# Moving two scale totals in the attention loop, and the load and split of the experts' second weight, in an attention and mixture-of-experts kernel

## The chip, the cores and the metric

The kernel runs on one core of a Trainium2 chip. The metric is device time in microseconds (us), as the median of several runs. The engines named below are TensorE (PE, with its weight loads as PEld), VectorE (DVE), ScalarE (ACT), GpSimd (POOL) and SyncE (SP); SP computes nothing here and issues most of the DMA transfers. Each engine works through its own list of instructions in order.

## The reference, cut to what matters

Eight batches of eight heads, 576 positions of 64 dimensions. Half of the heads see the last 32 positions, the other half see every 32nd position. The attention output, seen as 4608 tokens of 512 values, goes through a layer of eight experts, each of which takes exactly 576 tokens, in order of their gate logits over all experts.

```python
attn = np.exp(scores - max)                  # scores masked, scale 1/sqrt(64)
x = (attn / (attn.sum(-1) + 1e-9)) @ v       # -> [4608, 512]
logits = x @ w_gate                          # [4608, 8]
for idx in np.argsort(-logits.flatten()):    # best (token, expert) pair first
    tok, e = idx // 8, idx % 8
    if assigned[tok] >= 0 or counts[e] >= 576:
        continue
    assigned[tok] = e
    counts[e] += 1
for e in range(8):
    h = np.maximum(x[assigned == e] @ w1[e], 0.0)   # w1: 512 x 1024
    out[assigned == e] = h @ w2[e]                  # w2: 1024 x 512
```

## The kernel before

The kernel has two parts, one behind the other.

**Attention.** There are 16 units of work: for each batch one for the strided heads and one for the local heads, with two pairs of heads each. One loop of 33 steps (`for i in range(-1, 2 * nu)`, line 626) works on three pairs at a time: it closes the scores of pair i + 1, opens those of pair i + 2, and mixes and normalises pair i. Here the order of the instructions on every engine is that of the code (`tc.manual_schedule()`). The values are scaled by a power of two that comes from the sum of their squares: `square_v` squares them on ScalarE (line 292), `total_v` (line 294) adds them over the partitions with one small matmul into a PSUM bank and reduces it on VectorE, and `scale_v` (line 299) makes the power of two from it with six short VectorE operations. `norm` (line 397) multiplies by this scale. At the steps 2 and 4, for the first two batches, `total_v` and `scale_v` stand between `max_t` and the second `mix` of the step (lines 659 to 661).

**Experts.** For each of the eight experts, in an order that the data set (the expert that fills first is first), the kernel does the following:

- `search` or `rest` finds the expert and the bound of its logits, in seven rounds of short steps that go from VectorE to TensorE and back (lines 817 to 859);
- `weights` (line 976) reads the expert's number and loads both weights as four transfers each, issued on SP (line 985), into one buffer per weight (`wp`, `bufs=1`); the next expert's load of a weight waits until the last reader of that buffer is done;
- the weights are split into two halves of 16 bits: four squares on ScalarE (`square`, line 1000), a sum with one matmul and a few VectorE operations (`scale`, lines 1006 to 1009), then eight cuts, each one operation on ScalarE and one on VectorE (`split`, lines 1018 and 1019);
- `fetch` (line 1156) finds the token numbers (`indices`), gathers five tiles of token rows on POOL's queue (`tokens`, line 1078), halves them on ScalarE and VectorE and transposes them by DMA on SP (`halve`, lines 1067 to 1069);
- `ffn` (line 1185) multiplies: a hidden stage, the product with the first weight (`hidden`, line 1175, with the relu at 1182 and 1183), and an output stage, the product with the second weight (line 1223, and 1217 for the last 64 rows), whose result is scaled (line 1233) and scattered on POOL's queue (line 1234).

While expert k multiplies, the searching, loading, splitting and fetching for the experts behind it run beside it. TensorE's order is written out by hand: each matmul in `ffn` yields its planned nanoseconds, which advance `clock`; other work stands in `chains`, generators that yield the planned time to their next step, and the step is taken when the clock reaches it. Where it holds a matmul, that matmul then stands at that place of TensorE's order. The other engines are ordered by a scheduler, with `urgent` work first. A chain for the weights of an expert starts at `weights`: 4 us, the four squares of the first weight and its scale, then its cuts, with the squares of the second weight between the first four cuts, the second scale behind the sixth, and the cuts of the second weight at the end. When the multiplication of that expert begins, whatever is left of the chain is taken at once (`rush`, and `advance` in the loop at line 1271). Expert 0 has a path of its own.

## Time and profile before

| | |
|---|---|
| median of 3 runs | 678.89 us (674.91 to 679.88) |
| the profiled execution | 676.12 us |
| its span, from the first instruction to the last | 674.4 us |
| first matmul of expert 0's hidden stage | at 220.4 us |
| last matmul of expert 7's output stage | at 663.1 us |
| DMA | 102.40 MB, mean 152 GB/s |

Times in profile rows are microseconds from the span's start. A row of the timeline reads: start, length, engine, line, operation, output tile, input tiles, shapes, count; in brackets stands how long the engine was idle ahead of it and what ended the wait. A row of the table of stretches reads: stretch, length, busy time and count for each engine, granted clock of TensorE, mean busy share of the 16 DMA engines, and GB/s. The names of tiles are those of the code: `xt` holds transposed token rows, `xr` gathered rows, `w` a weight as loaded, `w1h`, `w1l`, `w2h`, `w2l` the halves, `r` and `g` belong to the search, `rv` to the token numbers.

### The profile page before, as it was taken

The numbers are of one execution on the slowest core, as the hardware profiler recorded it, in microseconds if no ns is written. First come the engines' busy times: TensorE is split into PE (matmuls) and PEld (weight loads), VectorE is DVE, ScalarE is ACT, GpSimd is POOL, SyncE is SP. The second block draws the span as 40 slices with busy tenths as digits, with TensorE's granted clock in tenths as the row PEclk, the third lists the DMA queues.
The fourth block names the chain that finished last, engine by engine and source line by source line (L and its number), as shares of the span: only waits on it lengthen the run. The fifth ranks groups of instructions, "written<-read, shape, count | busy, mean of one in ns | idle before, by whom it ended". The sixth has DMA issues, their size and how long they took to land.

```text
span 674.4 us, 19427 instructions
## 1 busy us (share of the span) xinstructions
PE 602.9 (89%) x8125; PEld 394.4 (58%) x8128; DVE 456.9 (68%) x1381; ACT 333.0 (49%) x554; POOL 110.8 (16%) x124
## 2 busy tenths in 40 slices
PE   7789899999847788999899989989989997999993
PEld 4567676776633564476467458447646744746741
DVE  4858787788787787777686786777768648570200
ACT  2555554555303464843851871664384279761210
POOL 2101101111102000500420430240042041211011
PEclk9959999999967799999999999989999999899997
DMA  8888798887406406803921860860491197911010
GB/s 240 200 231 222 209 241 239 246 234 215 137 2 216 129 1 236 209 17 131 268 63 35 299 129 1 286 160 17 174 245 44 67 306 228 240 35 48 1 40 32
DMA packets 76363, 102.40 MB, mean 152 GB/s; under 512 B 41292, under 2 KB 49062, under 8 KB 75763
## 3 DMA queue, kind: packets, MB, share of 16 engines
q1 hardware_dynamic: 68195, 79.61, 41.5%
q0 software_dynamic: 7360, 21.15, 10.4%
q8 instruction: 64, 1.05, 0.6%
q10 hardware_dynamic: 720, 0.39, 0.2%
q14 instruction: 24, 0.20, 0.1%
HBM read 73.60 MB, written 18.87 MB: 137 GB/s over the span
## 4 chain that ended last, share of the span: by engine, by line
PE 46%; issue 16%; DVE 15%; DMA 11%; ACT 6%; POOL 3%; SPq 1%; another core or an unknown queue 0%; POOLq 0%; ACTq 0%; DVEq 0%
PE ph L1175 17%; PE ph L1223 7%; PE po L394 4%; PE spa L351 4%; DMA w<-in_w_dram 4%; DMA xr<-x_scr,idx 2%; DVE w2l L1019 2%; DVE w1l L1019 2%; POOL xr L1078 2%; ACT jk L292 2%; DMA v_s<-in_ns_dram 2%; POOL out_dram L1234 1%; PE spb L469 1%; PE spa L374 1%; ACT w1h L1018 1%
## 5 line engine op out<-in xcount | busy, mean ns | idle before, releaser
L1175 PE MATMUL ph<-xt,w1h 128*128 128x288 f16 (+2 forms) x1024 | 177.9, 289 | 7.0 <-DMA xt<-xg 4.5
L1175 PEld LDWEIGHTS <-w1h 128*128 128x128 f16 x1024 | 97.7, 99 | 38.0 <-issue 8.5
L1175 PE MATMUL ph<-xt,w1l 128*128 128x288 f16 (+2 forms) x512 | 111.8, 289 | 0.0
L1234 POOL DMA_INDIRECT out_dram<-y,idx x40 | 47.8, 1195 | 337.2 <-ACT y L1233 314.6
L1223 PE MATMUL ph<-w2h,hh 128*128 128x512 f16 x256 | 97.8, 382 | 0.0
L1223 PE MATMUL ph<-w2h,hl 128*128 128x512 f16 x256 | 97.7, 382 | 0.0
L1223 PE MATMUL ph<-w2l,hh 128*128 128x512 f16 x256 | 97.5, 381 | 0.0
L1182 ACT ACTIVATE hh<-ph 128x576 f16<-128x576 f32 (+2 forms) x72 | 42.8, 595 | 108.6 <-PE ph L1175 108.0
L1000 ACT ACTIVATE jk<-w 128x1024 f16<-128x1024 f32 x64 | 67.4, 1053 | 57.8 <-DMA w<-in_w_dram 56.8
L1223 PEld LDWEIGHTS <-hh 128*128 128x128 f16 x512 | 49.4, 98 | 57.4 <-issue 7.2
L1183 DVE SCALAR_TENSOR_TENSOR hl<-ph,hh 128x576 f16<-128x576 f32 (+2 forms) x72 | 49.5, 687 | 43.7 <-ACT hh L1182 43.5
L1175 PEld LDWEIGHTS <-w1l 128*128 128x128 f16 x512 | 50.4, 99 | 13.3 <-issue 0.6
L1078 POOL DMA_INDIRECT xr<-x_scr,idx x40 | 41.6, 1040 | 51.2 <-DMA w<-in_w_dram 25.3
L377 ACT ACTIVATE pr<-spa 128x576 f32<-128x576 f32 x32 | 20.8, 651 | 57.6 <-PE spa L374 52.7
L1223 PEld LDWEIGHTS <-hl 128*128 128x128 f16 x256 | 25.1, 98 | 39.6 <-issue 14.8
L1019 DVE SCALAR_TENSOR_TENSOR w1l<-w,w_sw,w1h 128x512 f16<-128x512 f32 x64 | 45.6, 742 | 3.7 <-ACT w1h L1018 2.5
L1019 DVE SCALAR_TENSOR_TENSOR w2l<-w,w_sw,w2h 128x512 f16<-128x512 f32 x64 | 46.3, 744 | 2.1 <-ACT w2h L1018 2.0
L1018 ACT ACTIVATE w2h<-w,w_sw 128x512 f16<-128x512 f32 x64 | 41.1, 710 | 6.6 <-DVE w_sw L209 6.6
L1018 ACT ACTIVATE w1h<-w,w_sw 128x512 f16<-128x512 f32 x64 | 42.8, 709 | 3.0 <-DVE ss_e L204 1.8
L1233 ACT ACTIVATE y<-ph,so 128x512 f32<-128x512 f32 x32 | 21.8, 680 | 44.5 <-PE ph L1223 30.7
L428 POOL DMA_DIRECT2D x_scr<-xs x23 | 16.5, 724 | 154.0 <-DVE vsum L297 101.4
L394 PE MATMUL po<-v_s,pr 64*54 64x65 f32 x768 | 31.3, 230 | 2.4 <-DMA v_s<-in_ns_dram 1.5
(619 smaller groups left out, 920.3 us busy)
## 6 DMA issues: line engine op xcount, KB each, us to landing
w<-in_w_dram SPq DMA_DIRECT2D x64, 512.0 KB
kl<-in_kl_dram SPq DMA_DIRECT2D x16, 304.0 KB
v_s<-in_ns_dram SPq DMA_DIRECT2D x16, 292.5 KB
v_l<-in_nl_dram SPq DMA_DIRECT2D x16, 292.5 KB
ks<-in_ks_dram SPq DMA_DIRECT2D x16, 288.0 KB
qs<-in_qt_dram SPq DMA_DIRECT2D x16, 288.0 KB
ql<-in_qt_dram SPq DMA_DIRECT2D x16, 288.0 KB
x_scr<-xl SPq DMA_DIRECT2D x8, 512.0 KB
```

The source lines that it names most:

```text
L351: nc.tensor.matmul(u.sp[p][64 * f:64 * f + m, h, o:o + n], u.kt[r, p * u.nk + c:p * u.nk + c + m], u.q[r, p, c:c + n], start=False, stop=F ...
L394: nc.tensor.matmul(po[r:r + u.nq, j - j0], pr[k, o:o + u.nq], u.vn[k, t, 2 * p + h], start=(j == j0), stop=(j == j1 - 1), skip_group_check ...
L1000: nc.scalar.activation(jk, wf[:, c * n4:(c + 1) * n4].rearrange("p c f -> p (c f)"), AF.Square, scale=1.41422, accum_out=sq[:, c:c + 1])
L1018: nc.scalar.activation(hi[:, c, f], wf[:, c, f], AF.Copy, scale=s_)
L1019: nc.vector.scalar_tensor_tensor(lo[:, c, f], wf[:, c, f], s_, hi[:, c, f], op0=OP.mult, op1=OP.subtract)
L1078: nc.gpsimd.indirect_dma_start(out=xr[:n], out_offset=None, in_=x_rows, in_offset=bass.IndirectOffsetOnAxis(ap=idx[:n, t:t + 1], axis=0))
L1175: nc.tensor.matmul(tile_[:, j, :w], wt[:, d, f * 128:(f + 1) * 128], xt[:, d // 2, xx, d % 2, c], start=(k == 0), stop=(k == 3 * DC - 1))
L1182: nc.scalar.activation(hv, src, AF.Relu)
L1183: nc.vector.scalar_tensor_tensor(lv, src, 0.0, hv, op0=OP.max, op1=OP.subtract)
L1223: nc.tensor.matmul(py, a[:, f, ts_], w[:, f], start=(k == 0), stop=(k == len(todo) - 1))
L1233: nc.scalar.activation(y, py, AF.Copy, scale=so[:, t:t + 1])
L1234: st = nc.gpsimd.indirect_dma_start(out=out_rows, out_offset=bass.IndirectOffsetOnAxis(ap=idx[:n, t:t + 1], axis=0), in_=y[:n], in_offset= ...
```

## The change

In the attention loop the totals and scales at the steps 2 and 4 stand behind the second `mix` and the opened scores of the pair after next, just ahead of `norm`.

For the experts 1 to 7, `weights` issues the transfers of the first weight alone. Those of the second weight are issued in `fetch`, behind the last transpose of the token rows. The chain that starts at `weights` holds the first weight's squares, scale and cuts. The second weight's squares, scale and cuts form a chain of their own, which starts when the multiplication of that expert starts: 4 us, squares and scale at steps of 1.5 us, cuts at steps of 1 us. What is left of it is taken at the end of the hidden stage, ahead of the scale of the outputs.

```diff
+T_W21, T_CUT2 = 4000, 1000
...
-            if i in (2, 4):
-                mids2[i].total_v(b)
-                mids2[i].scale_v()
             if nu_ and i % 2 == 0:
                 nu_.load_v(1, n[0].top)
             elif kq_ and i % 2:
...
             if m:
                 open_scores(m)
             warm(i, 2)
+            if i in (2, 4):
+                mids2[i].total_v(b)
+                mids2[i].scale_v()
             if u:
                 u[0].norm(u[1])
...
+    thirds = {}
+
+    def evenly(todo):
+        for step, f in todo:
+            yield step
+            f()
...
-            k = W_EARLY if ph == 0 and name == "w2" else 4
+            k = 4 if name == "w1" else 0 if ph else W_EARLY
             fetch_w(range(k))
-            if k < 4:
+            if k == 0:
+                later = lambda go=fetch_w: go(range(4))
+            elif k < 4:
...
-        todo = [(T_W, lambda: None)] + sq1 + sc1
-        for a, b in zip(cut1[:4], sq2):
-            todo += [a, b]
-        todo += cut1[4:6] + sc2 + cut1[6:] + cut2
-        g = spread(ph, todo)
+        g = spread(ph, [(T_W, lambda: None)] + sq1 + sc1 + cut1)
         chains.append([due_now(), g])
-        return res, g
+        thirds[ph] = evenly([(T_W21, lambda: None)] + sq2 + sc2 + [(T_CUT2, f) for _, f in cut2])
+        return res, g, later
...
         for t, f in enumerate(todo):
             yield T_ROWS if t == 0 else T_ROW
             f()
+        wts[2]()
         yield T_LOAD - T_ROWS
...
-        for _ in second[0] if ph == 0 else ():
+        for _ in second[0] if ph == 0 else thirds[ph]:
             pass
...
+                if ph:
+                    chains.append([clock, thirds[ph]])
                 for cost in ffn(ph, *work[ph][:4]):
```

## The prediction

> **What bounds the kernel now.** I read the page's first part, then the busy table cut at the stages of the expert loop (the cuts are where line 1175 and line 1223 first run for each expert), then TensorE's timeline for every wait over 0.25 us.
>
> ```profile
> span 674.4 us, 19427 instructions
> PE 602.9 (89%) x8125; PEld 394.4 (58%) x8128; DVE 456.9 (68%) x1381; ACT 333.0 (49%) x554; POOL 110.8 (16%) x124
> ```
>
> The span is 674.4 us; this execution took 676.12 us, so 1.7 us lie around it. It is 2.8 us under the median of the three runs (678.89), inside their spread. My sum is made against 676.12.
>
> Columns of the next view: stretch, its length, busy time (count) of PE, PEld, DVE, ACT and POOL, granted clock, DMA share, GB/s.
>
> ```profile
> 285.50:312.20 26.70, 25.14 (x238) 20.17 (x237) 19.56 (x60) 10.33 (x17) 0.97 (x1) 1.00 0.08 19
> 312.20:342.00 29.80, 26.83 (x197) 12.89 (x196) 22.08 (x70) 20.20 (x34) 11.03 (x9) 1.00 0.84 247
> 342.00:367.60 25.60, 25.30 (x239) 20.19 (x238) 18.95 (x60) 10.06 (x16) 0.97 (x1) 1.00 0.05 17
> 534.80:560.10 25.30, 25.26 (x163) 11.62 (x161) 14.99 (x53) 17.61 (x31) 7.66 (x8) 1.00 0.89 277
> 560.10:592.10 32.00, 27.14 (x236) 20.48 (x235) 23.67 (x56) 26.50 (x46) 6.77 (x7) 0.95 0.83 229
> 615.90:639.40 23.50, 23.50 (x194) 18.77 (x193) 5.31 (x7) 5.25 (x8) 0.97 (x1) 1.00 0.04 13
> 332.00:340.00 8.00, 6.49 (x38) 2.98 (x38) 6.40 (x16) 6.05 (x11) 2.60 (x2) 1.00 1.06 215
> 318.00:324.00 6.00, 6.00 (x77) 3.26 (x74) 3.95 (x12) 5.81 (x11) 1.38 (x2) 1.00 1.03 390
> ```
>
> Rows one to six are hidden stage 1, output stage 1, hidden stage 2, output stage 5, hidden stage 6 and hidden stage 7 (experts counted from 0). TensorE is full in hidden stage 7 (23.50 of 23.50) and nearly so in hidden stage 2, where DMA is idle (0.05). Output stage 1 has 3.0 us without a matmul, hidden stage 6 has 4.9 and hidden stage 1 has 1.6. So the expert loop is bound by TensorE, and only its waits can be won. The largest that the change touches:
>
> ```profile
> 287.38 0.54 PE L1175 MATMUL ph<-xt,w1h 128*128 128x288 f16 x3 [1.56 <-DMA xt<-xg]
> 563.33 0.54 PE L1175 MATMUL ph<-xt,w1h 128*128 128x288 f16 x3 [2.92 <-DMA xt<-xg]
> 573.85 0.92 PE L961 MATMUL pr__9134<-ohl,rv 128*32 128x64 f16 x20 [1.95 <-DVE rv L947]
> 340.42 0.17 PE L842 MATMUL pr__5921<-r,fold 68*128 68x8 f16 x1 [0.86 <-DVE r L839]
> 395.24 0.17 PE L842 MATMUL pr__6686<-r,fold 68*128 68x8 f16 x1 [1.60 <-DVE r L839]
> 507.70 0.17 PE L842 MATMUL pr__8216<-r,fold 68*128 68x8 f16 x1 [0.85 <-DVE r L839]
> ```
>
> Two are token rows that come late, at the start of hidden stages 1 and 6; one is the slot search of the last expert; three are search steps held up by VectorE near the end of output stages 1, 2 and 4.
>
> **The totals (attention).** The same matmul, reduce and scale chain move behind the second mix and the opened scores. Nothing is added or removed. At i = 4:
>
> ```profile
> 34.30 0.30 PE L361 MATMUL spa<-ident,mx_s 128*32 128x64 f32 x4 [0.46 <-DVE mx_s L355]
> 35.63 0.19 ACT L292 ACTIVATION_READ_ACCUMULATOR jk<-v_l 64x1 bf16 x1
> 36.38 0.16 PE L295 MATMUL spb<-vsq,twos 128*128 128x2 bf16 x1 [1.78 <-ACT xt L458]
> 36.48 1.55 PE L394 MATMUL po<-v_s,pr 64*54 64x65 f32 x24
> 38.08 0.23 DVE L409 TENSOR_SCALAR rc<-po,ss_s 118x12 f32<-118x12 f32 x1 [0.45 <-PE po L394]
> 38.55 0.87 PE L351 MATMUL spa<-ql,kl 64*64 64x32 f32 x24
> 42.45 1.14 PE L449 MATMUL spb<-ident,xs 54*128 54x54 f32 x12
> ```
>
> TensorE stands 1.78 us in front of the total, with the mix queued behind it. After the change the mix starts at 34.6, and mix, masks and scores (36.48 to 38.55 + 0.87 = 39.42, so 2.94 us) are through at 37.5. The square is ready at 35.82 and the bank at about 36.4, so the total waits for nothing and the following matmuls come about 1.8 us earlier. What is late next is the norm: total to norm took 38.08 - 36.38 = 1.7 us with the mix between, and the scale chain alone is shorter, so the norm moves from 38.08 to about 38.8, 0.7 us later. Its output is first read by the transposes at 42.45, which would start at 40.7; the norm's 1.5 us of VectorE end at 40.3. That just fits. I take -1.5 us, between -1.8 and +0.7 (the norm's delay carried to the end).
>
> At i = 2 the wait is smaller, and behind it stands a copy that waits for a load:
>
> ```profile
> 23.59 0.16 PE L295 MATMUL spb<-vsq,twos 128*128 128x2 bf16 x1 [0.94 <-ACT jk L292]
> 28.82 0.18 DVE L547 COPY wgp<-wg_sb 128x32 f32<-128x32 f32 x1 [1.03 <-DMA wg_sb<-in_wg_dram]
> ```
>
> VectorE cannot pass 28.82 before that transfer lands, so 0.94 us won, or about half a microsecond lost on the norm, both end in this 1.03 us. Zero; without that cover -0.9 to +0.5.
>
> **The second weight (experts 1 to 7).** Four transfers on SP, four squares on ScalarE, a scale, eight cuts on ScalarE and VectorE; all stay, each later. The prices:
>
> ```profile
> L1000 ACT ACTIVATE jk<-w x64: 1039/1057/1062, 209.3 to 582.6; 128x1024 f16<-128x1024 f32 x64
> L1000 ACT ACTIVATION_READ_ACCUMULATOR jk<-w x64: 185/187/195, 210.3 to 583.6; 128x1 f32 x64
> L1018 ACT ACTIVATE w2h<-w,w_sw x64: 704/709/723, 243.9 to 604.6; 128x512 f16<-128x512 f32 x64
> L1019 DVE SCALAR_TENSOR_TENSOR w2l<-w,w_sw,w2h x64: 734/743/753, 244.7 to 605.5; 128x512 f16<-128x512 f32 x64
> ```
>
> Per expert: squares 4 x (1.057 + 0.187) = 5.0 us of ScalarE, leaving the output stage before; cuts 8 x 0.709 = 5.7 us of ScalarE and 8 x 0.743 = 5.9 us of VectorE, leaving the first ten microseconds of the hidden stage for the span from 12.5 to 19.5 us of its plan. Hidden stage 2 has 25.60 - 10.06 = 15.5 us of ScalarE free, so the squares fit there.
>
> *Queues.* SP's order, and three gathers as the chain of work shows them:
>
> ```profile
> 312.49 5.54 SPq L985 DMA_DIRECT2D w<-in_w_dram  x8
> 330.13 8.60 SPq L1069 DMA_TRANSPOSE xt<-xg  x5
> 551.55 8.63 SPq L1069 DMA_TRANSPOSE xt<-xg  x5
> 563.17 10.04 SPq L985 DMA_DIRECT2D w<-in_w_dram  x8
> 273.07 5.84 DMA xr<-x_scr,idx
> 384.94 3.54 DMA xr<-x_scr,idx
> 547.55 5.33 DMA xr<-x_scr,idx
> ```
>
> Of the eight transfers at 312.49 four go behind the five transposes, past five gathers on POOL's queue. Behind them SP next holds only the next expert's index and first weight, some 25 us later; their buffer has been free since the hidden stage before. The gathers at 273.07 and 547.55 took 2.3 and 1.8 us longer than the one at 384.94; the table's row for 318 to 324 shows what a weight load leaves (390 GB/s, share 1.03). For experts 1 and 6 the second weight is what is still under way. [...]
>
> *Hidden stage 1.* The gathers come 2 us sooner and the four squares no longer stand between the halvings on ScalarE: the 1.56 us go, -1.6 (0 to -1.6).
>
> *Hidden stage 6.* The same takes the 2.92. The cuts that fill VectorE at its start leave the slots of the last expert free, so the 1.95 us behind rv go too. Against it: the last expert's first weight now stands on SP behind expert 6's second weight, and its scale matmul is fixed in TensorE's order. I allow 1.5 us of new wait there, being the tail of its squares. -3.4, between -4.9 and 0.
>
> *Output stages 1 to 4.* The three search waits (0.86, 1.60, 0.85) have first-weight cuts of VectorE in front of them, which now run with no squares between. They may spread out, but their number stays: -1.0, between -3.3 and +1.0.
>
> *Hidden stages 1 to 5.* Eight cuts now meet the later search steps. In output stages such meetings cost 0.85 to 1.60; at the start of hidden stages, where the same cuts stand now, almost nothing (25.60 - 25.30). Nearest is the latter: +0.2 each, +1.0, from 0 to +5.
>
> *Stage 7 and expert 0.* Hidden stage 7 has 18 us of both engines free, so its cuts cost nothing; expert 0 is unchanged.
>
> Sum: -1.5 - 1.6 - 3.4 - 1.0 + 1.0 = -6.5 us, so 676.12 - 6.5 = **669.6 us**.
>
> **The rivals.**
>
> *Waits that come back.* The won waits reappear: 5 x 0.85 us at search steps beside the cuts, and a late norm (+0.7 in place of -1.5). That is -6.5 + (4.25 - 1.0) + 2.2 = -1.1, 675 us. For it speaks that VectorE has most of its time taken in every stage with a search (18.95 of 25.60); against it that the cuts cost little at the start of hidden stage 2.
>
> *Slower: the second weight too late.* Its scale matmul stands 11.5 us of plan into the hidden stage, in TensorE's fixed order; whatever it waits, the matmuls behind wait too, seven times. The transposes end near 339.5, the hidden stage starts at 342.0, and 2 MB at 390 GB/s take 5.4 us, so the data is there at about 346 and four squares end by 352, against 354 for the matmul. So 2 us of room. Lateness beyond that counts sevenfold: it turns my gain into a loss of 1% from (6.8 + 6.5) / 7 = 1.9 us each. With 3 us each the time is 669.6 + 21 = 690.6 us. The transposes speak for it: from 332 to 340 they hold the engines (share 1.06) at 215 GB/s, little over half of what the load reached. [...]
>
> *It doesn't do what it says.* If the weight lands no later for the gathers than before, only the attention term stays: 676.12 - 1.5 = 674.6 us. SP keeps its order, so I give this little.
>
> **How the numbers follow.** Forecast 0.50, waits that come back 0.30, no effect on the loads 0.08, too late 0.12. One per cent is about what a measurement of this kernel can tell from no change. The forecast's own range is 664 to 672.5: the low end takes each gain nearly whole (-1.8 - 1.6 - 4.9 - 3.3 = -11.6), the high end loses about half. The range of 664.0 to 677.5 takes in the second and third rival, and leaves out the late weight. Faster by over 1% needs 6.8 us, which the centre of the forecast just misses against 676.12 and clears against the median: 0.46. Within 1%: the other part of the forecast and two rivals, 0.42. Slower 0.12.
>
> **What would show it.** Right: no wait for xt at the start of hidden stages 1 and 6; no wait before the total at i = 4, and the transposes at 42.45 earlier by 1.5; second-weight transfers behind the transposes, squares over before the scale matmul. Wrong: waits of TensorE at line 1008 in hidden stages (too late), or new waits at lines 842 and 852 there (waits that come back).

## The result and the profile after

The changed kernel is a little slower. Its median is 683.79 us (677.52 to 691.48) against 678.43 us (674.48 to 685.87) for the kernel before beside it; the ratio is 1.0076, with a 95% interval of 1.0051 to 1.01. Two repetitions gave 1.0012 (0.9951 to 1.0073) and 1.0042 (1.0005 to 1.0079). The kernel before, run against itself, gave 0.9968 (0.9939 to 0.9996), so three parts in a thousand between two kernels tell nothing by themselves, even where the interval leaves out 1. Two of the three intervals lie above 1: the change loses, by something between 0.1% and 0.8%, where a gain of 1% was forecast. Ratios compare the executions within 1.5% of each kernel's fastest, while medians are of all executions (the first repetition's medians, 684.30 and 680.24 us, are 0.6% apart, its ratio 0.1%), and the profiles of e5, e9, e14 and e18 below are of executions longer than that.

First the head of the page of the changed kernel, and the stages that answer to those shown of before (stretch, length, busy time and count of PE, PEld, DVE, ACT and POOL, granted clock, DMA share, GB/s): output stage 0, hidden stage 1, output stage 1, hidden stage 6, output stage 6 and hidden stage 7.

```profile
span 681.4 us, 19422 instructions
256.80:290.60 33.80, 29.34 (x197) 13.42 (x194) 22.49 (x78) 19.52 (x34) 8.95 (x9) 0.90 0.73 223
290.60:316.30 25.70, 25.33 (x238) 20.03 (x237) 18.43 (x58) 10.02 (x16) 0.97 (x1) 1.00 0.03 11
316.30:346.10 29.80, 26.93 (x197) 12.85 (x195) 22.00 (x70) 19.98 (x34) 9.47 (x9) 1.00 0.84 252
564.70:596.30 31.60, 26.48 (x235) 20.14 (x234) 16.55 (x46) 18.99 (x34) 6.80 (x7) 0.95 0.59 159
596.30:622.80 26.50, 24.15 (x122) 10.53 (x120) 10.59 (x17) 15.10 (x25) 4.09 (x4) 1.00 0.32 115
622.80:646.40 23.60, 23.60 (x195) 18.82 (x194) 11.25 (x21) 10.02 (x16) 0.97 (x1) 1.00 0.03 12
```

The same view of the kernel before, for the two stages of these that the prediction did not show, output stages 0 and 6:

```profile
256.10:285.50 29.40, 26.67 (x196) 12.65 (x194) 21.59 (x75) 19.23 (x34) 9.99 (x9) 1.00 0.86 248
592.10:615.90 23.80, 23.80 (x124) 10.64 (x122) 11.26 (x21) 10.31 (x17) 4.19 (x4) 1.00 0.11 39
```

Hidden stage 1 is 1.0 us shorter, as forecast in direction. Output stage 1 and hidden stage 7 have not moved. Two places lost time: output stage 6 grew by 2.7 us, with TensorE busy 24.15 of 26.50 us where it had been full, and output stage 0 by 4.2 us, at a mean clock of 0.90. Hidden stage 6, where half of the gain was expected, kept its length. TensorE's waits in the changed kernel say why (timeline; the last bracket is the wait and what ended it):

```profile
279.72 0.17 PE L850 MATMUL pr__5070<-r,fold 68*128 68x8 f16 x1 [3.52 <-DVE r L847]
566.17 0.54 PE L1183 MATMUL ph<-xt,w1h 128*128 128x288 f16 x3 [1.23 <-DMA xt<-xg]
578.64 1.50 PE L969 MATMUL pr__9101<-ohl,rv 128*32 128x64 f16 x36 [3.90 <-DVE rv L955]
600.08 0.38 PE L1231 MATMUL ph<-w2l,hh 128*128 128x512 f16 x1 [0.79 <-DVE w2l L1029]
601.40 0.38 PE L1231 MATMUL ph<-w2l,hh 128*128 128x512 f16 x1 [0.52 <-DVE w2l L1029]
602.73 0.38 PE L1231 MATMUL ph<-w2l,hh 128*128 128x512 f16 x1 [0.52 <-DVE w2l L1029]
604.05 0.38 PE L1231 MATMUL ph<-w2l,hh 128*128 128x512 f16 x1 [0.52 <-DVE w2l L1029]
```

In expert 6 the wait for token rows fell from 2.92 to 1.23 us, but the one behind `rv` doubled from 1.95 to 3.90 us, and four new waits, 2.35 us together, stand where the output stage needs the second weight's halves. That is -1.69 + 1.95 + 2.35 = +2.6 us, and the two stages together went from 55.7 to 58.2 us. Hidden stage 6 kept its length because one wait took the place of the other (4.87 us together before, 5.13 after); the stage that grew is the output stage.

SP's own timeline shows that the load did not move, except for the last expert:

```profile
539.07 5.03 SPq L993 DMA_DIRECT2D w<-in_w_dram  x8
555.64 7.95 SPq L1076 DMA_TRANSPOSE xt<-xg  x5
566.24 2.27 SPq L993 DMA_DIRECT2D w<-in_w_dram  x4
586.85 7.75 SPq L1076 DMA_TRANSPOSE xt<-xg  x5
604.03 2.11 SPq L993 DMA_DIRECT2D w<-in_w_dram  x4
```

Both weights of expert 6 still go out as eight transfers at 539.07, 16 us ahead of its transposes; only those of expert 7 come as four, the transposes, and four. The code asks for the second weight's load last, but SP is not ordered by hand. A transfer that waits for nothing was put ahead of transposes that wait for data; so it is for experts 1 to 6. What really changed for them is only when the second weight is squared and cut.

How that hurts expert 6 is told by ScalarE and VectorE of the changed kernel, from the end of output stage 5 to the cuts. ScalarE first: `jk` are squares, `hh` is the first ReLU of the hidden stage.

```profile
570.20 1.06 ACT L1010 ACTIVATE jk<-w 128x1024 f16<-128x1024 f32 x1 [4.50 <-DMA w<-in_w_dram]
571.25 0.67 ACT L1241 ACTIVATE y<-ph,so 128x512 f32<-128x512 f32 x1
...
574.05 0.63 ACT L1190 ACTIVATE hh<-ph 128x576 f16<-128x576 f32 x1
```

The square at 570.20 is the first of expert 7's first weight, whose transfers SP issued only at 566.24. It stands ahead of `y` and `hh` and waits 4.50 us for its data, and they wait with it. In the kernel before the second weight's cuts stood in that place of ScalarE's list (563.7 to 569.2 us), with the first ReLU among them, and the squares came behind:

```profile
563.70 3.17 ACT L1018 ACTIVATE w2h<-w,w_sw 128x512 f16<-128x512 f32 x5 [0.82 <-DVE w_sw L209]
566.78 0.63 ACT L1182 ACTIVATE hh<-ph 128x576 f16<-128x576 f32 x1
...
569.15 1.05 ACT L1000 ACTIVATE jk<-w 128x1024 f16<-128x1024 f32 x1
```

VectorE of the changed kernel:

```profile
574.71 0.76 DVE L1191 SCALAR_TENSOR_TENSOR hl<-ph,hh 128x576 f16<-128x576 f32 x1 [8.49 <-ACT hh L1190]
...
577.93 0.66 DVE L955 TENSOR_TENSOR rv<-ohh,val 128x972 f16<-128x972 f16 x1
...
585.11 0.16 DVE L205 TENSOR_SCALAR ss_e<-pr__9203 128x1 int32<-128x1 int32 x1 [2.43 <-PE pr__9203 L1018]
...
590.81 0.69 DVE L1075 TENSOR_TENSOR xg<-xr,xg 128x512 f16<-128x512 f32 x1 [1.22 <-ACT xg L1074]
591.42 0.15 DVE L207 TENSOR_SCALAR ss_e<-ss_e 128x1 int32<-128x1 int32 x1
```

VectorE is idle for 8.49 us behind that ReLU, with expert 7's slots and `rv` in the list behind it: hence the 3.90 us. Then the scale of expert 6's second weight begins at 585.11 and its next small step comes at 591.42, behind four halvings (`xg`) that wait for expert 7's gathers one by one. The cuts run from 592.6 to 603.3, past the start of the output stage at 596.3. Before, the eight cuts were done at 571.

### The profile page after: what moved, and what is told of

It reads as the page before. It is cut to its first block, busy times and chain, and to the rows that moved or that the text cites. A ratio compares the mean times of both kernels' runs of the same rounds, so it can differ in the third digit from the quotient of the medians.

```text
span 681.4 us, 19422 instructions
## 1 busy us (share of the span) xinstructions
PE 603.3 (89%) x8125; PEld 393.6 (58%) x8128; DVE 454.6 (67%) x1381; ACT 333.1 (49%) x554; POOL 106.2 (16%) x124
## 4 chain that ended last, share of the span: by engine, by line
PE 45%; DVE 20%; issue 16%; DMA 9%; ACT 5%; POOL 2%; SPq 1%; another core or an unknown queue 0%; ACTq 0%; POOLq 0%; DVEq 0%
PE ph L1183 13%; PE ph L1231 10%; PE po L395 5%; PE spa L352 5%; DMA w<-in_w_dram 4%; DVE w2l L1029 3%; DVE w1l L1029 2%; DVE hl L1191 2%; DMA xt<-xg 2%; PE spa L375 1%; DVE xg L1075 1%; PE spb L470 1%; POOL out_dram L1242 1%; DVE cm L825 1%; DVE v_l L328 1%
## 5 line engine op out<-in xcount | busy, mean ns | idle before, releaser
L1242 POOL DMA_INDIRECT out_dram<-y,idx x40 | 45.3, 1133 | 349.5 <-ACT y L1241 328.2
L1085 POOL DMA_INDIRECT xr<-x_scr,idx x40 | 40.2, 1004 | 47.8 <-DVE L L934 25.3
L1075 DVE TENSOR_TENSOR xg<-xr,xg 128x512 f16<-128x512 f32 (+1 forms) x37 | 25.7, 693 | 14.8 <-ACT xg L1074 9.6
```

Of the source, the lines that this page charges most:

```text
L1075: nc.vector.tensor_tensor(xs[:, 1], xv, xs[:, 0], op=OP.subtract)
L1085: nc.gpsimd.indirect_dma_start(out=xr[:n], out_offset=None, in_=x_rows, in_offset=bass.IndirectOffsetOnAxis(ap=idx[:n, t:t + 1], axis=0))
L1242: st = nc.gpsimd.indirect_dma_start(out=out_rows, out_offset=bass.IndirectOffsetOnAxis(ap=idx[:n, t:t + 1], axis=0), in_=y[:n], in_offset= ...
```

## The experiments

Seventeen runs in five groups (e1, e2, e4 and e5; e6 to e9; e10 to e12; e13 to e15; e16 to e18), each group on one chip with the kernel before beside it. A ratio is always to the kernel before of its group, with its 95% interval. The stages are of one profile each.

| kernel | ratio (interval) | hidden + output stage 6, us | output stage 0, us |
|---|---|---|---|
| before | 1 | 55.7 | 29.5 |
| changed | 1.0076 (1.0051 to 1.01) | 58.2 | 33.7 |
| e1 totals alone | 0.9985 (0.9946 to 1.0024) | 55.8 | 27.9 |
| e2 weight alone | 1.0037 (1.0001 to 1.0074) | 59.6 | 28.8 |
| e4 weight, not expert 6 | 0.9948 (0.9904 to 0.9991) | 55.3 | 28.6 |
| e5 weight, expert 6 alone | 1.0132 (1.0075 to 1.019) | not read | 28.6 |
| e6 both, not expert 6 | 0.9974 (0.9943 to 1.0005) | 55.9 | 28.6 |
| e7 load really behind | 1.01 (1.0061 to 1.014) | 59.0 | 28.4 |
| e8 scale of expert 6 first | 0.997 (0.9939 to 1.0) | 55.2 | 28.6 |
| e9 expert 7's squares later | 0.9914 (0.9886 to 0.9942) | 54.2 | 28.9 |
| e10 changed, again | 1.0012 (0.9951 to 1.0073) | 58.8 | 33.3 |
| e11 both repairs | 0.9962 (0.9926 to 0.9999) | 51.3 | 34.0 |
| e12 repairs, totals as before | 0.9961 (0.9924 to 0.9998) | 51.1 | 34.1 |
| e13 before, again | 0.9968 (0.9939 to 0.9996) | 55.5 | 29.3 |
| e14 changed, third | 1.0042 (1.0005 to 1.0079) | 58.7 | 32.9 |
| e15 both repairs, again | 0.9979 (0.9933 to 1.0026) | 53.3 | 31.6 |
| e16 changed, 48 fills | 1.0092 (1.0051 to 1.0134) | 59.3 | 33.3 |
| e17 repairs, 48 fills | 1.0028 (0.9987 to 1.0069) | 53.5 | 33.6 |
| e18 changed, fourth | none | 58.8 | 33.0 |

**Which part costs: e1 and e2.** e1 is the move of the two totals alone, e2 all the rest of the diff.

> Only the two totals are moved; the experts are as before. Theory (the loss is made in expert 6): no loss here, 0 to -1.5 us against before, ratio 0.998 to 1.000. Rival (the moved totals cost the 1.8 us by which the attention part was longer in the profile after): about +1.8 us, ratio 1.0027. In the profile, the start of expert 0's hidden stage would then stand near 222.2 instead of 220.4.

> Only the second weight's load and split are moved; the attention part is as before. Theory (loss made in expert 6): +4 to +6 us, ratio 1.006 to 1.009, with TensorE waiting for rv in hidden stage 6 and for w2l at the start of output stage 6. Rival (the totals): +2 to +3.5 us, ratio 1.003 to 1.005.

e1 took 674.36 us against 677.68, e2 679.41. No cost of the totals is to be seen; the weight's change costs something. The 1.0037 of e2 lies below its theory's range and in its rival's, but its profile has the theory's waits, 3.94 us behind `rv` and 2.19 us on `w2l`, which the totals do not touch. In e1 the forecast step can be seen, on TensorE at step 4:

```profile
34.69 0.30 PE L361 MATMUL spa<-ident,mx_s 128*32 128x64 f32 x4 [0.48 <-DVE mx_s L355]
...
36.77 0.16 PE L295 MATMUL spb<-vsq,twos 128*128 128x2 bf16 x1
...
39.68 0.72 PE L449 MATMUL spb<-ident,xs 54*128 54x54 f32 x12 [0.97 <-DVE xs L412]
```

The total waits for nothing (1.78 us before), and the transposes now wait 0.97 us for the output of the norm (`xs`), which the working had fit just in time. From line 361 to the transposes it takes 39.68 - 34.69 = 5.0 us, where it took 42.45 - 34.30 = 8.2 us; the granted clock, 0.50 from 36.4 to 42 us in the kernel before, is 1.00 here, which is part of that. Nor does the kernel before always wait there; in its second profile (e13) the same total stands without a wait:

```profile
38.45 0.16 PE L295 MATMUL spb<-vsq,twos 128*128 128x2 bf16 x1
```

**Which expert: e4 and e5.** Both have the attention of before. e4 gives expert 6 alone its old path; e5 gives the new path to expert 6 alone.

```diff
+LATE = (1, 2, 3, 4, 5, 7)          # e5: (6,)
-            k = 4 if name == "w1" else 0 if ph else W_EARLY
+            k = 4 if name == "w1" or ph and ph not in LATE else 0 if ph else W_EARLY
...
-        g = spread(ph, [(T_W, lambda: None)] + sq1 + sc1 + cut1)
+        todo = [(T_W, lambda: None)] + sq1 + sc1
+        if ph in LATE:
+            todo += cut1
+        else:
+            for a, b in zip(cut1[:4], sq2):
+                todo += [a, b]
+            todo += cut1[4:6] + sc2 + cut1[6:] + cut2
```

> The second weight is loaded and split late for experts 1 to 5 and 7, as before for expert 6; attention as before. Theory (loss made in expert 6): no loss, and the 1.6 us of hidden stage 1 won, -2 to 0 us, ratio 0.997 to 1.000; hidden stage 6 and output stage 6 as long as before (32.0 and 23.8 us). Rival (each expert pays for the cuts beside the search): +3 us or more, ratio 1.004 or more.

> The second weight is loaded and split late for expert 6 alone. Theory (loss made in expert 6): +2.5 to +6 us, ratio 1.004 to 1.009, with the waits for rv and w2l of the changed kernel. Rival (each expert pays): under +1 us, ratio under 1.0015.

673.52 and 685.48 us: leaving expert 6 out turns the loss into a gain of 0.1 to 1.0%, and expert 6 alone makes the largest loss. Both ratios lie outside their theory's range, e4 below it and e5 above. e5 is not a clean isolation, for expert 7's old path behind expert 6's late cuts adds a wait of its own (9.18 us at expert 7's scale matmul). e2 and e4 differ in expert 6 alone, by 0.9%; that settles the place on this chip, where output stage 0 is not longer (28.8 and 28.6 us).

**The same with the totals: e6.** The edit of e4 on the whole changed kernel.

> Both parts of the change, but expert 6's second weight goes the old way: its load issued with the first weight's, its squares and cuts between the first weight's. Theory (the whole loss is made in expert 6's stages, and both other parts are worth something or nothing): below the kernel before, at 0.9985 * 0.9948 = 0.993 of it, 0.989 to 0.997; hidden stage 6 at 31.7 us and output stage 6 at 23.5 us as in the kernel with the weight's change alone and expert 6 left out. Rival (the two parts disturb each other: with the totals moved, something of the attention's gain or of experts 1 to 5's is lost): at 0.998 or above.

671.75 us, 0.9974: expert 6's output stage no longer waits for `w2l`, and no loss is left. The 0.993 of the theory and the 0.998 of its rival both touch the interval, so this run does not tell them apart. The wait behind `rv` was 3.77 us here and 1.31 in e4, whose order differs by the totals alone; the wait for token rows ahead of it was 1.47 and 2.96 us. So on the old path much of what TensorE does not wait for the rows it waits behind `rv`. In the changed order the wait behind `rv` is near 3.9 us in every profile (3.90, 3.94, 3.94, 3.94, 3.93 in the changed kernel, e2, e10, e14 and e18), with waits for rows from 1.23 to 1.86 us.

**Is it the place of the load? e7** orders the transfers of each second weight behind the transposes of its expert on SP.

```diff
-                    nc.sync.dma_start(wf[:, c * n4:c * n4 + n4], src[:, c * n4:c * n4 + n4])
+                    ld = nc.sync.dma_start(wf[:, c * n4:c * n4 + n4], src[:, c * n4:c * n4 + n4])
+                    for tr in turned.get(ph, ()):
+                        tc.add_manual_dep(ld.ins, tr.ins.name, NOSYNC, reason="rows first")
...
-            nc.sync.dma_start_transpose(xt[:, :, t * 128:t * 128 + n], xg[:n])
+            turned.setdefault(ph, []).append(nc.sync.dma_start_transpose(xt[:, :, t * 128:t * 128 + n], xg[:n]))
```

> The changed kernel, with an order between each second weight's transfers and the row transposes of its expert added on SP, so that for experts 1 to 6 too the transfers really stand behind the transposes (in the changed kernel they still stood ahead: 539.07 against 555.64 us for expert 6). Theory (the place of the load has nothing to give: its packets have drained by 556 us, when the transposes' begin, so the xt waits come of the gathers and halvings ahead of them): the xt wait in hidden stage 6 stays at 0.8 us or more, and since expert 6's second weight now shares the wires with expert 7's first at 566 us, expert 7's squares come later, the rv wait of 3.9 us does not shrink, and the time is that of the changed kernel or up to 15 us longer: 1.005 to 1.03 of the kernel before. Rival (the prediction's: transposes that need not share with the weight end earlier): the xt wait of 1.23 us in hidden stage 6 goes, hidden stages 1 to 5 keep their 25.6 us, and the time is 1 to 3 us below the changed kernel's, 1.003 to 1.006.

679.51 us, 1.01. The wait for token rows at the start of hidden stage 6 did go, so that half of the first theory fell. But the time is longer, and expert 6 is not the only one that pays. SP, TensorE and, around hidden stage 2, ScalarE and VectorE of e7:

```profile
549.86 7.66 SPq L1079 DMA_TRANSPOSE xt<-xg  x5
557.72 5.76 SPq L994 DMA_DIRECT2D w<-in_w_dram  x8
```

```profile
351.59 0.47 PE L842 MATMUL pr__6077<-ohn,cm 128*68 128x32 f16 x9 [1.68 <-DVE cm L826]
...
575.69 1.51 PE L970 MATMUL pr__9101<-ohl,rv 128*32 128x64 f16 x36 [5.28 <-DVE rv L956]
```

```profile
349.22 1.06 ACT L1013 ACTIVATE jk<-w 128x1024 f16<-128x1024 f32 x1 [0.94 <-DMA w<-in_w_dram]
```

```profile
350.40 0.16 DVE L1019 TENSOR_REDUCE ss<-sq 128x1 bf16<-128x4 f32 x1 [1.33 <-ACT jk L1013]
350.48 0.23 DVE L864 SCALAR_TENSOR_TENSOR cand<-steps,pr__5997,pre 128x18 f32<-128x18 f32 x1
```

The last square waits for its data, the sum of squares (`ss`) waits for the square, and the next search step (`cand`) stands behind that sum in VectorE's list; so TensorE waits 1.68 us for `cm`. Hidden stages 1 to 5 took 28.7, 27.4, 27.3, 26.4 and 27.8 us in e7, against 25.6 or little more. The output stages 1 to 4 were shorter, 28.4 to 28.6 us against 29.0 to 29.3 in e8, which won back less than a third of that. The load's place takes away the 1.2 us in front of hidden stage 6, but TensorE then waits 5.28 us behind `rv` and the stage is no shorter (32.1 us), and it costs some 1 to 3 us in each hidden stage whose search stands behind the late squares.

**Two repairs of expert 6: e8 and e9.** e8 gives the scale and cuts of expert 6's second weight the halvings' priority. e9 puts the squares of expert 7's first weight behind the second ReLU of hidden stage 6 and starts their chain later (14 us in place of 4).

```diff
+        def first_(f):                                          # e8
+            with urgent() if ph == E - 2 else nullcontext():
+                f()
+        # sc2 and cut2 of thirds[ph] go through first_
...
-        g = spread(ph, [(T_W, lambda: None)] + sq1 + sc1 + cut1)
+        g = spread(ph, [(T_W7 if ph == E - 1 else T_W, lambda: None)] + sq1 + sc1 + cut1)    # e9
...
+                if first_of == (E - 1, "w1") and HH_AHEAD:                                   # e9, in square
+                    tc.add_manual_dep(a.ins, relus[FC * (E - 1) + HH_AHEAD - 1].ins.name, NOSYNC, reason="hidden first")
```

> The changed kernel with one thing set right: expert 6's second weight's scale and cuts get the high priority that the halvings have, so that they stand ahead of four of expert 7's five halvings on VectorE and ScalarE; TensorE's, SP's and POOL's orders are the changed kernel's. Theory (output stage 6's 2.35 us are the scale behind the halvings, which wait for gathers): the four waits on w2l go, output stage 6 falls from 26.5 to 23.5 to 24.3 us, the rv wait of 3.9 us in hidden stage 6 stays, hidden stage 7 starts without a wait of over 1.5 us, and the time is 2 to 3 us below the changed kernel's: 1.0035 to 1.0055 of the kernel before. Rival (the cuts are late because expert 7's cuts share ScalarE and VectorE with them, not because of the halvings): waits on w2l of 1 us or more in all stay, and the time is within 1 us of the changed kernel's.

> The changed kernel with the squares of expert 7's first weight put behind the second ReLU of expert 6's hidden stage on ScalarE (in the changed kernel the first of them stands ahead of the first ReLU and waits 4.5 us for its data). Its chain starts later for it, so expert 6's second weight is squared and cut earlier too. Theory (the 3.9 us at rv is the ReLU behind that square, and VectorE's work for expert 7 behind the ReLU): ScalarE waits for no weight ahead of the first ReLU, the rv wait falls from 3.9 to 2 us or less, and the waits on w2l in output stage 6 shrink or go with the earlier cuts: 2 to 4.5 us below the changed kernel, 1.001 to 1.005 of the kernel before. Rival (rv is late from the search and the slots of expert 7, not from the ReLU): the rv wait stays at 3.5 us or more while ScalarE no longer waits.

In e8 (670.95 us) output stage 6 is full again and the wait behind `rv` stays, 3.94 us. Its hidden and output stage 6:

```profile
555.50:587.20 31.70, 26.50 (x236) 20.04 (x235) 18.45 (x45) 21.46 (x38) 6.79 (x7) 0.95 0.57 152
587.20:610.70 23.50, 23.50 (x122) 10.57 (x120) 9.27 (x19) 12.65 (x22) 3.88 (x4) 1.00 0.48 138
```

So the 2.35 us were the scale behind the halvings: nothing else in TensorE's, SP's or POOL's order changed. In e9 (668.40 us) ScalarE's first two ReLUs wait for TensorE alone, and no wait behind `rv` of 0.25 us or more is left:

```profile
569.88 0.65 ACT L1194 ACTIVATE hh<-ph 128x576 f16<-128x576 f32 x1 [4.40 <-PE ph L1187]
572.88 0.65 ACT L1194 ACTIVATE hh<-ph 128x576 f16<-128x576 f32 x1 [2.35 <-PE ph L1187]
```

The waits on `w2l` went with it, since the chain of expert 7 that now starts later let expert 6's second weight be squared and cut earlier. Both rivals fell. Both ratios lie below their forecast ranges; a likely reason is that those were counted from 1.0076, which held a longer output stage 0 that this chip did not have (below).

**The two repairs together, and the changed kernel again: e10, e11, e12.** e11 is e8 and e9 together, e12 the same with the totals where they were before.

> The changed kernel itself, not altered, for a second profile of it and a second ratio. Theory (the loss is in expert 6: 2.3 us of w2l waits and 2 us of the longer rv wait, less 1.7 us of the shorter xt wait, so 2.4 us in its two stages together; what the first profile had beside it, 1.8 us of attention and 4.2 us of output stage 0 with its wait of 3.52 us, is scatter): the waits on w2l in output stage 6 and the rv wait of 3.9 us in hidden stage 6 stand as before to within 0.3 us, the wait of 3.52 us in output stage 0 is gone or below 1.5 us, the ratio to the kernel before is 1.003 to 1.006, and the span from the first matmul of hidden stage 1 to the end is 390 to 393 us (the kernel before 388.9). Rival (output stage 0's wait belongs to the change): it stands again, and the ratio is 1.0075 or more.

> The changed kernel with both repairs of expert 6: the squares of expert 7's first weight behind the second ReLU of hidden stage 6, and the scale and cuts of expert 6's second weight at the halvings' priority. Theory (the two waits are all that the change lost there, and they add): no rv wait of over 2 us, no waits on w2l, hidden and output stage 6 together 52.5 to 54.2 us (changed kernel 58.2, before 55.8), ratio to the kernel before 0.988 to 0.994, and 0.983 to 0.989 of the changed kernel of this call. Rival (the second repair takes from expert 7 what it gives expert 6: its halvings and its cuts come later): hidden stage 7 begins with a wait on xt or w1l of 1 us or more, and the time is no shorter than with the squares' repair alone, 0.9914.

> The same with the totals of squares where the kernel before has them, so that only the second weight's change with both repairs is left. Theory (the totals are worth 0 to 2 us, as the kernel with the totals alone showed by its 0.9985, interval 0.9946 to 1.0024): 0.998 to 1.003 times the time of the same kernel with the totals moved, of which 0.9985 was the ratio: 0.989 to 0.996 of the kernel before. Rival (the totals' move costs, which is why the changed kernel lost more than its second weight alone did, 1.0076 against 1.0037): this kernel is the shorter one, by 2 us or more.

Hidden and output stage 6 of e11:

```profile
561.90:589.70 27.80, 25.45 (x236) 19.79 (x235) 17.54 (x41) 18.99 (x34) 6.71 (x7) 1.00 0.74 180
589.70:613.20 23.50, 23.50 (x122) 10.55 (x120) 8.92 (x20) 12.55 (x21) 3.89 (x4) 1.00 0.43 135
```

51.3 us together: 7.5 less than in the changed kernel on the same chip (58.8) and 4.4 less than in the kernel before. Hidden stage 7 began without a wait. The wait for token rows is 2.35 us in e11 and 2.15 to 2.98 us in the other kernels with this order of the squares (e9, e12, e15, e17), so what the changed kernel won there is given back. The gain over the kernel before is the wait behind `rv` and the stretch of slow clock that followed it (the granted clock of hidden stage 6 is 0.95 before and 1.00 in e11). The medians are 677.89 us against 684.30 (changed), 6.4 us less; by the two ratios it is 0.5%, or 3.4 us. How much of the 7.5 us reaches the time is not known better than that. Against the kernel before both kernels missed their forecasts, e12 by little; their output stage 0 is some 4.5 us longer than in its first profile. e11 and e12 agree in time (0.9962 and 0.9961), so the totals' move is worth nothing that can be seen. And e10 refuted half of its theory: the wait of 3.5 us in output stage 0 was there again, with a ratio below both forecasts.

**Output stage 0: e13, e14, e15.** The kernel before, the changed kernel and e11 on one further chip.

> The kernel before itself, for a second profile of it beside those of the changed kernel on one chip. Theory (output stage 0's wait of 3.5 us, seen in four profiles with the weight's change and missing in five others, comes and goes with the run and the chip, whatever the kernel): either this profile too shows it on a chip where the changed kernel does, or it shows a wait of VectorE on the same kind of releaser in another output stage, as its first profile did at 443 us; ratio 1.000 within 0.004. Rival (it belongs to the changed order): output stage 0 is 29 to 30 us here while the changed kernel's in this call is 33 us or more.

> The changed kernel once more, for the size of its loss, which two calls gave as 1.0076 (1.0051 to 1.01) and 1.0012 (0.9951 to 1.0073). Theory (expert 6's two stages lose 2.4 to 3.1 us, the totals and experts 1 to 5 gain or lose less than 2): hidden and output stage 6 take 58 to 59 us together, the ratio is 1.002 to 1.006. Rival (something of 5 us or more belongs to the change besides expert 6): 1.0075 or more, and hidden stages 0 to 5 with output stages 0 to 5 take 3 us or more longer than in the kernel before's profile of this call.

> The changed kernel with both repairs once more, beside the changed kernel and the kernel before. Theory: hidden and output stage 6 take 51.3 us again, 7 us less than in the changed kernel and 4.4 us less than before; 0.990 to 0.996 of the kernel before, and 0.985 to 0.993 of the changed kernel of this call. Rival (what expert 6 gains is lost again behind it): hidden stage 7, output stage 7 and the tail take over 1 us more than the 58.5 us that they take in both kernels.

The rows of the search step in output stage 0, of e10, e13 and e8 in that order:

```profile
277.22 0.17 PE L850 MATMUL pr__5070<-r,fold 68*128 68x8 f16 x1 [3.46 <-DVE r L847]
```

```profile
275.79 0.17 PE L842 MATMUL pr__5074<-r,fold 68*128 68x8 f16 x1 [0.39 <-DVE r L839]
```

```profile
276.69 0.17 PE L850 MATMUL pr__5070<-r,fold 68*128 68x8 f16 x1 [0.74 <-DVE r L847]
```

The wait is no scatter of single runs. On the chips of the last three groups, and in the changed kernel's first profile, every profile of the changed order shows it (3.36 to 3.57 us), while the kernel before does not, on one of these chips (e13) and in its first profile. On the chips of the first two groups no kernel shows it, with the same order (e2, e4 to e9). The theory that it comes whatever the kernel fell, as far as two profiles of the kernel before can tell; at this place it takes the changed order and something that differs between chips. e14 met its forecast. e15 took 673.50 us, 8.3 less than e14 (681.78), by the ratios 0.6% or 4.3 us; against the kernel before its interval holds 1, and its stages of expert 6 took 53.3 us where 51.3 were forecast, with 2.75 us of waiting for token rows.

The trace's semaphores tell more. TensorE waits there for `r`, which VectorE makes behind the reduction `red` (line 844), and `red` waits for a semaphore that TensorE's matmuls alone count up (628 of them in the changed kernel's first profile, and no other instruction). The count that it needs, that of the search's last matmul, came 3.8 to 4.1 us behind this matmul's recorded end in all nine profiles that show the wait, and 0.01 or 0.02 us behind it in e2 and e4 to e9. (The ends of matmuls are modelled in the profile.) So VectorE waited for TensorE's count, and TensorE in its turn for VectorE. The chips differ in this for every kernel: in the first profiles of both kernels and in all of the last three groups, e13 included, 15 to 25 of some 627 counts of this semaphore are missing from the record, and in the other eight profiles none.

**What it hangs on: e16, e17, e18.** 48 small fills lengthen VectorE's list early in the kernel.

```diff
         nc.vector.memset(wgp, 0.0)
+        for _ in range(48):
+            nc.vector.memset(peak[:, 4:], 2.0 ** -101)
```

> The changed kernel with 48 small fills of one tile (128x1) added on VectorE at about 5 us, where it waits for TensorE anyway; every engine's order is otherwise the changed kernel's. It asks what output stage 0's wait of 3.5 us hangs on. In all six profiles that show it the search's reduction stands at the same place of VectorE's list, number 723 of its rows (725 with the totals moved back), and waits 1.7 to 2.7 us for something outside the core's engines. Theory (it hangs on how far VectorE's list has been read, as with a fetch of instructions): with the list 48 longer the wait at this reduction goes, output stage 0 falls to 28.4 to 29.5 us, a like wait may stand elsewhere, and the ratio to the kernel before is 2 to 5 us lower than that of the changed kernel of this call. Rival (it hangs on the data or on the moment): the same reduction waits again, 1.5 us or more, output stage 0 is 31.5 us or more, and the time is that of the changed kernel.

> The changed kernel with both repairs of expert 6, and the 48 small fills. Theory (the two repairs and the fills add): output stage 0 28.4 to 29.5 us, hidden and output stage 6 51 to 53.5 us, 0.985 to 0.992 of the kernel before, below both kernels. Rival (the fills only move the wait to another stage): a wait of 1.5 us or more on the same releaser in another output stage, and the time is that of the kernel with the repairs alone, 0.996 to 0.998.

> The changed kernel, not altered, as the measure for the two kernels with the fills on the same chip: where its output stage 0 shows the wait (32 us or more), their result tells; where it does not (28 to 29 us), they leave the question open. By theory 1.002 to 1.006 of the kernel before; by the rival that the wait makes up half the loss, 1.001 to 1.004 without it and 1.005 to 1.008 with it.

The changed kernel on that chip (e18) showed the wait, 3.55 us, and so did e16 and e17, at the same reduction (3.57 and 3.48 us). Its place in VectorE's list is not the cause, and both theories fell. The two kernels have further waits of the kind, of VectorE ahead of the same line: e16 1.73 us in output stage 3 and 3.10 us in output stage 4 (which took 32.5 us), e17 1.69 us in output stage 2. e16 took 684.75 us and e17 678.42, 6.3 less (by the ratios 0.6%, or 4.3 us): the repairs' worth a third time, though e17 does not beat the kernel before there. For e18 there is no ratio; its median is 683.85 us against 679.08.

## Why the prediction was wrong

**Hidden stage 6 (-3.4) is the step that failed.** It said that "the cuts that fill VectorE at its start leave the slots of the last expert free, so the 1.95 us behind rv go too". VectorE was free indeed, and idle for 8.49 us: the slots stood behind the low half of the first ReLU, the ReLU stood on ScalarE behind a square, and the square waited for data. Moving work off VectorE did not help, because ScalarE's order had changed with it; e9 shows this by changing that order. The 2.92 us went partly (1.23 left), to no use: `rv` was ready 13.9 us after the start of the stage, 13.7 us before the change. For new waits 1.5 us were allowed; 2.35 us came, in the four waits on `w2l`, in output stage 6, and from a scale held up by halvings, not from the square's tail in TensorE's order. Forecast -3.4 us; both stages together measured 58.2 - 55.7 = +2.5 in the first pair of profiles and 58.8 - 55.5 = +3.3 in the second (e10, e13). That is an error of some 6 us, the largest of all.

**"SP keeps its order" failed too.** The sum took the written order for SP's real one. For experts 1 to 6 the load did not move. For expert 1 it was not in the way either: the last packet of its weights ended at 272.85 us in the kernel before, and the gather that was said to run beside it began at 273.07 (for expert 6 the weights ended at 551.11, behind the gather of 547.55). And e7, where the load really moved, was no faster. So the rival "it doesn't do what it says", given 0.08, was right about the load and wrong in thinking that then nothing but the attention term remains: squares and cuts had moved all the same. A smaller misreading stands beside this: the stretch from 332 to 340 us, read as transposes at 215 GB/s, holds gathers too. From 558 to 562 us of the changed kernel, with transposes alone, it is 188 GB/s at a DMA share of 0.98, which only strengthens what was drawn from it.

**Expert 0 "is unchanged"** held for its code and not for its time: output stage 0, in which expert 1's weights and rows are prepared, was 3.4 to 4.2 us longer in the changed kernel wherever the wait of 3.5 us stood. No term of the sum looked there. Not all of it need reach the end: from the first matmul of expert 0 to that of expert 6 the kernel before took 339.8 us and the changed one 342.4 in the first pair, but 341.8 and 340.9 in e13 and e14.

**Hidden stage 1 (-1.6)** was right in direction: 26.7 to 25.7 us in the first pair, 28.1 to 25.9 in e13 and e14. On a chip without the longer output stage 0 ahead of it, 0.82 and 0.86 us of its wait stayed (e2, e4); with the load where it was, this gain cannot be the load's.

**Output stages 1 to 4 (-1.0)**: 120.3 us before and 121.7 in e13, against 119.7, 122.0, 118.2 and 120.7 in the four profiles of the changed kernel, each as the sum of the four. A gain of 1 us cannot be told from this scatter; the search waits are spread out and not fewer, as the text allowed.

**Hidden stages 2 to 5**: 102.2 us before, 102.8 after. The meetings of cuts and search steps cost even less than the +0.2 each: three of the four stages grew by 0.02 to 0.08 us, and the fourth, stage 3, by 0.5 us, with a wait of 0.31 us for token rows. In stage 3 single profiles lose more to late rows (e2 takes 29.4 us there, e16 28.4).

**The totals (-1.5)** did in part what the working said, at its place: the wait of 1.78 us is gone, but the transposes wait for the norm (0.97 us in e1). And the term rested on a wait of one profile, which the second profile of the same kernel does not have. No gain at the end is shown: 0.9985 (0.9946 to 1.0024) alone, and no difference between e11 and e12.

**The slower rival** had the right kind of cause, second-weight work that is late, with the wrong multiplicity: not seven times at the scale matmul, but once, at the expert behind which the last expert has no search to space it out (SP issues expert 7's first weight at the start of hidden stage 6, those of the experts before in output stages). Something like it appears in e7, where the load really stands behind the transposes: all of the hidden stages 1 to 5 grow, though at search steps behind the late squares and not at the scale matmul.

What stays open is why TensorE's count comes late in output stage 0, and why on some chips only; the changed kernel itself was not run on the two chips that do not show it. And since the ratios of the changed kernel run from 1.0012 to 1.0076, the loss is known in sign better than in size.

## What to carry to other kernels

Where a scheduler orders an engine, moving a step in the program is a request: read the order it made for every engine, queues too, before costing the move. When work is taken from the front of a busy engine, ask what the next instruction in that list waits for, since a short operation on the critical path behind one that waits for a transfer inherits the whole wait (here a ReLU of 0.63 us behind a square that waited 4.50 us). Where a wait has no releaser among the engines, look whose instructions count its semaphore up. And look apart at the last but one round of a pipeline, where the neighbours that spaced the work out in the other rounds are missing.

## What the runs showed of the hardware

A wait whose end the profile calls remote need not come from outside the core. In the changed kernel's output stage 0 this stood ahead of an operation whose matmuls had ended at 274.7 by their rows:

```profile
276.28 0.74 DVE L1075 TENSOR_TENSOR xg<-xr,xg 128x512 f16<-128x512 f32 x1
278.70 0.19 DVE L844 TENSOR_TENSOR red<-pr__5070,fold 68x32 f16<-68x32 f32 x1 [1.68 <-remote]
```

The semaphore that it waits for is counted up by TensorE's matmuls alone. The counts of the matmuls that end at 274.68 and 276.20 by the record came together, at 278.68 and 278.76 us, and the next one, of a matmul that ends at 279.88, at 279.90; in e9 each came within 0.02 us of the recorded end. Whether these matmuls ended late or only their counts did, the trace does not tell. The kernel before had one such wait in its first profile, 1.67 us long and ended at 443.11, and none in its second.

Two waits of TensorE were paid for twice, since a stretch of slow clock came with them. At the one of 3.52 us that ended at 279.72, from 278.3 on, the table of stretches gives the granted clock as 0.51 for 6.9 us, and in the kernel before, after its wait of 2.53 us at 444.1, as 0.50 for 3.4 us. Not every wait was followed by one: after the wait of 2.92 us at 563.33 in the kernel before the clock stayed at 1.00 until 575.1. The two stretches:

```profile
278.30:285.20 6.90, 5.48 (x15) 1.97 (x15) 4.13 (x12) 1.64 (x4) 0.00 (x0) 0.51 0.66 133
```

```profile
445.40:448.80 3.40, 3.40 (x11) 1.20 (x10) 3.40 (x9) 2.82 (x6) 0.51 (x1) 0.50 1.11 247
```

Of the 5 us by which output stage 0 was longer than in e8, some 2.8 are the wait (3.52 against 0.74), and the rest fits the slow clock behind it, with 5.48 us of matmuls in that stretch, where those of 128x512 start 0.43 us apart, against 0.21 or 0.22 us just behind it. What sets the clock the traces do not show. The length of the wait alone does not, for 2.53 us came with a slow stretch here and 2.92 us with none in the 11.8 us behind it. The clock differs between two runs of one kernel too: in the attention part the kernel before had a granted clock of 0.53 from 42 to 50 us in its first profile and 1.00 in its second. And the first expert's first matmul came anywhere between 215.2 and 225.0 us over all profiles but e5's (231.3): more scatter than the change was worth.
